# Row-group scores, one-tile mixing and two-tensor work on VectorE in a linear-attention, Fourier-mixing and feed-forward kernel

## The chip, the core and the metric

The kernel runs on one core of one Trainium2 chip. A core has five engines, each with its own instruction queue that is worked off strictly in order: TensorE (PE in the profile; its weight loads are listed apart as PEld), VectorE (DVE), ScalarE (ACT), GpSimd (POOL) and SyncE (SP), from whose queue most transfers are issued. [...] The metric is the device time of one execution in microseconds (us), lower is better.

## The reference

For 4 batches and 8 heads of width 48 a state of 48 x 48 is carried over 768 tokens; the result is mixed by a two-dimensional Fourier transform, normalised and sent through a feed-forward network:

```python
def _attn_ref(q, k, v, alpha):
    ...
    for t in range(S):
        state = alpha[:, :, t, :, None] * state + np.einsum('bhd,bhe->bhde', k[:, :, t], v[:, :, t])
        y[:, :, t] = np.einsum('bhd,bhde->bhe', q[:, :, t], state)

def _moe_ref(x, w_ch1, w_ch2):
    X = np.fft.fft(np.fft.fft(x, axis=1), axis=2)
    u = x + np.real(X)
    un = (u - mean(u)) / np.sqrt(var(u) + 1e-06)
    return u + np.maximum(un @ w_ch1, 0.0) @ w_ch2
```

Here `x` is the attention result with its 8 heads side by side: 768 tokens by 384. `w_ch1` is 384 x 1536, `w_ch2` 1536 x 384. Everything is float32.

## The kernel before

**Attention.** The 32 (batch, head) problems run as 16 pairs of two heads, four pairs to a batch. The two heads of a pair lie on rows 0 to 47 and 64 to 111 of the 112 used rows. For a pair, `attn_stages` gives these stages: `s1` makes running products of alpha by two scans on VectorE (tiles `al` and `w`, the latter being tag `w3`) and a product `first` of 112x384; `s2` and `s3` multiply them by k and q (`times`, two products of 112x768); `s4` transposes the k side (`kt`); `s5` makes the scores, k against q, in chunks of 128 tokens; `s6` makes and chains the states between chunks (`tt`); `s7` multiplies scores by v and adds the carried state; then `combine` does the first radix-3 step of the Fourier transform along tokens (tiles `sd`, then six parts `z`).

**Scores in two forms.** Pairs 0 to 6 (`pair < FR`, FR = 7) use `s5`: float32 matmuls of one head each, on 64 or 48 rows of the array. Pairs 7 to 15 use `s5r`: k and q are each split into a high and a low part in the one-pass float32r format (tile `qs`), q also masked by head (`hm`), and three matmuls on all 112 rows with both heads side by side (128x256) make a chunk. `s5r` costs ScalarE three and VectorE three instructions for each half of a pair ahead of the matmuls. Either way ScalarE copies the scores out of PSUM and GpSimd zeroes the upper triangle (`affine_select`).

**Mixing, norm, feed-forward.** `mix_stages` folds the six parts of `z` (`f2`; z lies in three `w3` tiles of two parts each, so each step of the fold is issued three times), transforms along tokens (`mk_s`) and channels (`mk_d`) on TensorE, and VectorE adds the results to `y`. `norm_stages` normalises, transposes on TensorE (`n2`), and splits into high and low parts `x`. `ffn_stages` runs 12 blocks of 128 hidden channels for each of two halves of a batch: 9 float32r matmuls 128x384 (`f<-x,wt`; order lists them as `f<-x,wt` or `f<-wt,h` with moving and fixed operand exchanged), ScalarE's relu, VectorE's low part, 9 matmuls back. The two halves of 4 batches make 1728 matmuls. The weights are turned from float64 words to float32r high and low parts on the chip (`wsplit`).

**What sets the order.** All instructions are first collected with a key, then `Plan.emit` places them one at a time: it simulates five clocks with the costs in `duration`, the latencies `LAT`, a port rule for VectorE and GpSimd (`port`, `held`, `SHARE`) and takes, on the engine that can start earliest, the ready instruction with the lowest key. Some operations may go to either of two engines (`FX`, with a bias `SLACK`). The order so found is each engine's queue; on the chip nothing is reordered. In the first 120 us of its own clock the plan fills TensorE's gaps with dummy matmuls on a zero tile (`f<-zero`), one for each 0.11 us of gap. Tiles come from numbered slots of a tag (`w3`: NW3 = 8, `qs`: 3, PSUM `a`: 3, `f1`: 2, `f2`: 3); taking a slot waits for its last user. Of batch 1, MIX and K1 place some stages among the mixing of batch 0, ahead of the first feed-forward.

## Time and profile before

| | |
|---|---|
| runs, median (lowest to highest) | 571.66 us (571.16 to 576.05), 3 runs |
| the profiled execution | 572.74 us, of which the trace's span 570.9 us and 1.84 us around it |
| mean granted TensorE clock | 0.946 |
| busy: PE, DVE, ACT, POOL | 534.1, 398.2, 195.6, 220.1 us |
| GpSimd's instructions | 255, of which 175 TENSOR_TENSOR and 64 affine selects |

The profiled execution is 1.08 us above the median of the runs. A busy TensorE is not TensorE at its peak: matmuls overlap in the pipe, dummies count as busy, and the clock was 0.5 in parts of the first 100 us. So the profile has to be read by stages: first until the first feed-forward matmul, then while feed-forward and the next batch's attention share the engines, and last the feed-forward of the last batch alone.

### The profile page before, as it was taken

The numbers are of one execution on the slowest core, as the hardware profiler recorded it, in microseconds if no ns is written. First come the engines' busy times: TensorE is split into PE (matmuls) and PEld (weight loads), VectorE is DVE, ScalarE is ACT, GpSimd is POOL, SyncE is SP. The second block draws the span as 40 slices with busy tenths as digits, with TensorE's granted clock in tenths as the row PEclk, the third lists the DMA queues.
The fourth block names the chain that finished last, engine by engine and source line by source line (L and its number), as shares of the span: only waits on it lengthen the run. The fifth ranks groups of instructions, "written<-read, shape, count | busy, mean of one in ns | idle before, by whom it ended". The sixth has DMA issues, their size and how long they took to land.

```text
span 570.9 us, 10199 instructions
## 1 busy us (share of the span) xinstructions
PE 534.1 (94%) x4018; PEld 510.9 (89%) x4018; DVE 398.2 (70%) x903; ACT 195.6 (34%) x428; POOL 220.1 (39%) x255
## 2 busy tenths in 40 slices
PE   7999879989898999998989999999999999999995
PEld 6888878978887989998979999988999999999995
DVE  7766796898999666999984679989755932412111
ACT  3354422345643522245643213255522121211110
POOL 2557584264758440055857202358770000000000
PEclk8575976999998999999999999999999999999998
DMA  8999080230200250112324300221011100100001
GB/s 223 276 363 270 21 284 15 75 95 1 69 2 2 70 153 1 47 37 78 97 64 142 124 1 1 91 64 29 2 56 29 42 1 0 43 0 27 17 0 48
DMA packets 16550, 42.23 MB, mean 74 GB/s; under 512 B 1904, under 2 KB 7088, under 8 KB 16496
## 3 DMA queue, kind: packets, MB, share of 16 engines
q1 hardware_dynamic: 15440, 39.08, 22.2%
q0 software_dynamic: 768, 2.36, 1.4%
q8 instruction: 34, 0.56, 0.4%
q14 instruction: 20, 0.16, 0.1%
q10 hardware_dynamic: 288, 0.07, 0.1%
HBM read 34.42 MB, written 7.08 MB: 73 GB/s over the span
## 4 chain that ended last, share of the span: by engine, by line
PE 62%; DVE 18%; POOL 7%; DMA 4%; issue 4%; ACT 2%; SPq 1%; POOLq 0%; ACTq 0%; DVEq 0%
PE f L464 42%; PE a L464 19%; DVE w L464 6%; POOL w L464 4%; DMA al<-in_alpha_dram 4%; DVE al L464 3%; POOL sd L464 2%; DVE h L464 2%; PE f L1146 2%; DVE qs L464 2%; DVE x L464 2%; DVE tt L464 1%; DVE y L464 1%; DMA scr<-y 1%; SPq L464 1%
## 5 line engine op out<-in xcount | busy, mean ns | idle before, releaser
L464 PE MATMUL f<-wt,h 128*128 128x384 f32 x864 | 178.4, 342 | 5.1 <-DVE h L464 5.1
L464 PE MATMUL f<-x,wt 128*128 128x384 f32 x864 | 179.0, 343 | 0.8 <-DVE x L464 0.8
L464 PEld LDWEIGHTS f<-wt,h 128*128 128x128 f32 x864 | 149.9, 188 | 7.8 <-DVE h L464 7.2
L464 PEld LDWEIGHTS f<-x,wt 128*128 128x128 f32 x864 | 152.0, 189 | 1.8 <-DVE x L464 1.2
L464 DVE SCALAR_TENSOR_TENSOR h<-f,h 128x384 fp32r<-128x384 f32 x96 | 53.1, 553 | 93.2 <-ACT h L211 92.2
L211 ACT ACTIVATE h<-f 128x384 fp32r<-128x384 f32 x96 | 47.1, 490 | 182.3 <-PE f L464 176.4
L464 POOL TENSOR_SCALAR_AFFINE_SELECT w<-w 128x512 f32<-128x512 f32 (+1 forms) x64 | 47.5, 765 | 44.3 <-ACT w L464 44.3
L464 POOL TENSOR_TENSOR w<-w,rec 112x384 f32<-112x384 f32 (+1 forms) x17 | 18.1, 1065 | 103.3 <-DVE mt L464 45.5
L464 PE MATMUL a<-vn,w 128*128 128x64 f32 x312 | 49.4, 288 | 3.3 <-POOL w L464 2.3
L464 PEld LDWEIGHTS a<-vn,w 128*128 128x128 f32 x312 | 45.1, 208 | 5.3 <-POOL w L464 3.5
L464 POOL TENSOR_TENSOR sd<-y,y 128x288 f32<-128x288 f32 x32 | 33.0, 1052 | 35.6 <-ACT y L464 30.8
L1146 PE MATMUL f<-zero 128*32 128x32 f32 x798 | 36.8, 210 | 3.5 <-ACT w L464 1.9
L464 ACT COPY w<-a 128x512 f32<-128x512 f32 (+6 forms) x58 | 26.2, 481 | 40.2 <-PE a L464 39.0
L1146 PEld LDWEIGHTS f<-zero 128*32 128x32 f32 x798 | 32.8, 125 | 7.6 <-ACT w L464 2.4
L464 DVE TENSOR_TENSOR y<-y,a 128x191 f32<-128x191 f32 (+2 forms) x96 | 28.6, 346 | 13.3 <-PE a L464 13.1
L464 DVE SCALAR_TENSOR_TENSOR tt<-tt,mt 112x96 f32<-112x96 f32 x64 | 35.5, 557 | 0.3
L464 PE MATMUL a<-cst,w 96*128 96x96 f32 (+10 forms) x267 | 34.2, 267 | 1.3 <-DVE w L464 1.2
L464 PEld LDWEIGHTS a<-cst,w 128*96 128x96 f32 (+7 forms) x267 | 32.0, 166 | 3.2 <-DVE w L464 2.2
L464 DVE TENSOR_TENSOR_SCAN al<-al,d 112x768 f32<-112x768 f32 (+1 forms) x17 | 34.6, 2037 | 0.1
L464 PE MATMUL a<-qs,qs 112*128 112x256 f32 x162 | 29.2, 292 | 4.7 <-DVE qs L464 4.7
L464 DVE TENSOR_TENSOR_SCAN w<-al,d 112x768 f32<-112x768 f32 (+1 forms) x17 | 32.3, 1902 | 0.2
L464 PE MATMUL a<-tt,w 112*128 112x96 f32 x134 | 30.4, 312 | 1.1 <-DVE d L464 1.1
(129 smaller groups left out, 737.5 us busy)
## 6 DMA issues: line engine op xcount, KB each, us to landing
kq<-in_kq_dram SPq DMA_DIRECT2D x13, 672.0 KB, 5.4
wt<-in_w_dram SPq DMA_DIRECT2D x8, 768.0 KB, 10.9
al<-in_alpha_dram SPq DMA_DIRECT2D x15, 336.0 KB, 9.7
out_dram<-y SPq DMA_DIRECT2D x24, 192.0 KB, 1.9
vn<-in_v_dram SPq DMA_DIRECT2D x14, 296.0 KB, 3.5
wt<-in_w_dram SPq DMA_DIRECT2D x8, 384.0 KB, 13.0
scr<-y SPq DMA_DIRECT2D x4, 576.0 KB, 3.9
wt<-in_kq_dram SPq DMA_DIRECT2D x2, 672.0 KB, 12.7
```

Source lines behind the costliest of these rows:

```text
L211: return lambda out, x: e.activation(out, x, AF.Relu)
L464: op.ins = op.fns[op.engine](*[real(a) for a in op.args], **{k: real(x) for k, x in op.kwargs.items()})
L1146: plan.idle = (lambda: nc.tensor.matmul(warm[2][0:32, 480:512], zero.real(), zero.real(), start=True, stop=True), 1.0, WARM, ("f2", 2))
```

## The change

- `s5r`, FR and the tag `qs` go; all 16 pairs use `s5`. In the plan a float32 matmul on at most 64 rows costs a fifth less (750 for 600).
- `combine`, `times` (`mul`) and `first` are given to VectorE alone. The weights' products (`wm`, `wd`) may still go to either engine, now with no slack for GpSimd.
- `z` becomes one tile of six parts, and so does the folded `f`: each step of the fold is one instruction over six parts in place of three over two. The blk-0 norm result uses `f` too. NW3 falls from 8 to 5.
- In the plan VectorE and GpSimd no longer slow one another by a share: an instruction with two wide SBUF inputs (or a constant) waits until the other engine's has ended.
- In the plan a matmul that is no feed-forward (`not u.fill`) counts its operands from other engines as ready MARGIN = 1.0 us later than the latencies say.

```diff
-NQS = 3
-FR = 7
-NW3 = 8
+NW3 = 5
+MARGIN = 1.0
...
-                return max(m, slow * n) / 600 + 0.004
+                p0, p1 = self.region(named["1"])[0:2]
+                return max(m, slow * n) / (750 if p1 - p0 <= GRP else 600) + 0.004
...
         if len(wide) > 1:
-            return "part"
-        return "whole" if wide and op.name in ("tensor_scalar", "tensor_copy", "copy") and "scalar1" in named else None
+            return True
+        return len(wide) > 0 and "scalar1" in named and not isinstance(named["scalar1"], View)
...
+        def finish(op, e):
+            t = max(clock[e], start(op, e))
+            return (max(t, held[other[e]]) if op.port and e in held else t) + op.durs[e]
...
-                op.dur += (SHARE if op.port == "part" else 1.0) * both
...
+                op.dur += max(0.0, held[other[op.engine]] - t)
+                held[op.engine] = t + op.dur
...
+                    if e == "PE" and op.engine != "PE" and not u.fill:
+                        lat += MARGIN
...
-SLACK = {'ACT': 2.0, 'DVE': 0.5, 'POOL': 5.0}
-FX = {'comb': 'G', 'mul': 'VG', 'first': 'G', 'wm': 'VG', 'wd': 'VG', ...
-SHARE = 0.5
+SLACK = {'ACT': 2.0, 'DVE': 0.5, 'POOL': 0}
+FX = {'comb': 'V', 'mul': 'V', 'first': 'V', 'wm': 'VG', 'wd': 'VG', ...
...
-        "qs": ([P, 776], F32R, NQS), "sd": ...
+        "z": ([P, 6, DM], F32, 1), "f": ([P, 6, DM], F32, 1), "sd": ...
...
-        def s5r():
...
-        return [s1, s2, s3, s4, s5 if pair < FR else s5r, s6, s7, lambda: combine(...)]
+        return [s1, s2, s3, s4, s5, s6, s7, lambda: combine(...)]
...
-        z = [x[:, c0 : c0 + w] for x in zt[0]]
+        z = [zt[:, i, c0 : c0 + w] for i in range(6)]
...
-            for z, f in zip(zp, fp):
-                ze, zo = f[:, :, 0 : HM + 1], f[:, :, HM:DM]
-                E.tensor_add(ze[:, :, 1:HM], z[:, :, 1:HM], z[:, :, DM - 1 : HM : -1])
...
+            z, f = zt, plan.tile("f")
+            ze, zo = f[:, :, 0 : HM + 1], f[:, :, HM:DM]
+            E.tensor_add(ze[:, :, 1:HM], z[:, :, 1:HM], z[:, :, DM - 1 : HM : -1])
...
-                uw = [plan.tile("qs").bitcast(F32) if state["start"] else w3() for _ in range(2)]
+                uw = plan.tile("f")
```

The instruction counts follow: VectorE gains 32 `sd` (128x288) and 96 `z` (128x96) two-tensor instructions of `combine`, 19 products with k or q (18 of 112x768, one of 112x384), 17 `first` and 10 products of 128x768 of the weights; it loses 54 instructions with `qs` and two thirds of the fold's. GpSimd keeps the 64 `affine_select`, the 12 gathers and one weight product. ScalarE loses 54 instructions with `qs`. On TensorE 162 matmuls `a<-qs,qs` become 108 of `a<-w,al`.

The first place is the start-up, where the first pair of batch 0 is combined. Names are tiles with their buffer numbers: `sd`, `y`, `al`, `w` (tag `w3`), `d` (the scans' second input). On GpSimd's queue before:

```order
L464 TENSOR_TENSOR w_5_6_71<-w_5_6_71,rec 112x6x64
L464 TENSOR_TENSOR w_5_6_71<-wt_0_65_130,w_5_6_71 112x768
L464 TENSOR_TENSOR sd_13_78<-y_23_88,y_24_89 128x288 x2
L464 TENSOR_TENSOR w_6_7_72<-sd_13_78 128x96
L464 TENSOR_TENSOR w_7_8_73<-sd_13_78 128x96
L464 TENSOR_TENSOR w_6_7_72<-sd_13_78,w_6_7_72 128x96
L464 TENSOR_TENSOR w_3_92_515<-sd_13_78 128x96 x2
L464 TENSOR_TENSOR w_7_8_73<-sd_13_78,w_3_92_515 128x96
L464 AFFINE_SELECT w_0_93_517<-w_0_93_517 128x384 x2
```

The same work on VectorE's queue now, ahead of the scan of the fourth pair:

```order
L465 TENSOR_TENSOR al_38_103<-wt_0_61_126,al_38_103 112x768
L465 TENSOR_TENSOR sd_9_74<-y_19_84,y_20_85 128x288 x2
L465 TENSOR_TENSOR z_7_72<-sd_9_74 128x96 x2
L465 TENSOR_TENSOR z_7_72<-sd_9_74,z_7_72 128x96
L465 TENSOR_TENSOR z_7_72<-sd_9_74 128x96
L465 SCALAR_TENSOR_TENSOR z_7_72<-z_7_72,sd_9_74 128x96
L465 TENSOR_TENSOR z_7_72<-sd_9_74 128x96
L465 TENSOR_TENSOR z_7_72<-sd_9_74,z_7_72 128x96
L465 SCALAR_TENSOR_TENSOR w_1_91_536<-al_39_104,d_137 112x768
L465 SCALAR_TENSOR_TENSOR z_7_72<-z_7_72,sd_9_74 128x96
```

The combination stands between VectorE's own scans now, and GpSimd's queue goes from one `affine_select` to the next.

The second place is ScalarE's queue ahead of the first feed-forward matmul (`r` are the norm's small tiles, `x` the feed-forward's input, `c` and `bad` belong to the check of a later pair's alpha, `mh` and `y` to later pairs' states and results). Before:

```order
L464 ACTIVATE r_4_38_103<-mv_33_98,ceps 128x3
L464 ACTIVATE mh_136<-mt_140,hm 112x5 x2
L464 COPY y_27_92<-f_0_162_1123 128x3x96
L464 ACTIVATE c_0_183_1355,bad<-al_180_1307,cm_144 112x768
L464 COPY w_2_188_1371<-f_1_165_1148 128x384
L464 COPY w_2_188_1371<-f_0_171_1174 128x384
L464 COPY w_0_190_1398<-f_1_167_1156 128x384
L464 CAST x_191_1400<-f_1_189_1394 128x384
```

And now:

```order
L465 ACTIVATE r_1_31_96<-mv_28_93,ceps 128x3
L465 ACTIVATE r_4_34_99<-mv_29_94,ceps 128x3
L465 CAST x_146_1264<-f_0_143_1248 128x384
L465 CAST x_147_1267<-f_0_144_1250 128x384
L465 CAST x_150_1281<-f_1_145_1252 128x384
L465 ACTIVATE x_151_1285<-b_0_113_727 128x768
```

The states, results and the check of pairs 5 and 6 no longer stand ahead of the casts of `x`; they come after the feed-forward has begun. In TensorE's queue 212 attention and mixing matmuls (and 472 dummies) stand ahead of the first feed-forward matmul now, 273 (and 396) before.

The third place is TensorE's queue at the scores of one of the later pairs. Before (pair 7, float32r, both heads in one matmul):

```order
L464 MATMUL a_276_1901<-tt_134,w_1_178_1295 128x2x48
L464 MATMUL a_286_1970<-qs_12_77,qs_284_1960 128x256
L464 MATMUL a_286_1970<-qs_281_1937,qs_284_1960 128x256
L464 MATMUL a_288_1976<-qs_12_77,qs_284_1960 128x256
L464 MATMUL a_288_1976<-qs_281_1937,qs_284_1960 128x256
```

And now (pair 8, float32, one head on its own rows in each; two heads in turn write two PSUM tiles, or one head stands alone):

```order
L465 MATMUL a_376_2638<-w_4_317_2275,al_168_1348 128x128 x2
L465 MATMUL a_377_2642<-w_4_317_2275,al_168_1348 128x128 x2
L465 MATMUL a_378_2649<-w_4_317_2275,al_168_1348 128x128 x3
L465 MATMUL f_0_372_2618<-x_355_2539,wt_0_118_768 128x384
L465 MATMUL a_380_2658<-w_4_317_2275,al_168_1348 128x128 x3
L465 MATMUL a_383_2667<-vn_284_2050,kt_375_2631 112x96 x5
```

Over the nine later pairs 54 of the 108 score matmuls stand next to one of the other head, 54 alone, in 23 groups between other work.

More of the change, by code (lines that the diff above doesn't have):

```diff
@@ L328, in port @@
         if op.engine == "POOL":
-            return None if "dma" in op.name else "part"
-        if op.engine != "DVE" or op.name == "memset":
-            return None
+            return "dma" not in op.name
+        if op.name == "memset":
+            return False
         inputs = [a for k, a in named.items() if k != "out" and isinstance(a, View)]
@@ L365, in emit @@
         order = []
-        held = {"DVE": (0.0, 0.0), "POOL": (0.0, 0.0)}
+        held = {"DVE": 0.0, "POOL": 0.0}
+        other = {"DVE": "POOL", "POOL": "DVE"}
         def start(op, e):
@@ L396, in emit @@
                     if len(op.engines) > 1:
-                        done = max(now, t) + op.durs[e] - SLACK[e]
-                        if any(max(clock[o], start(op, o)) + op.durs[o] < done for o in op.engines if o != e):
+                        if any(finish(op, o) < finish(op, e) - SLACK[e] for o in op.engines if o != e):
                             continue
@@ L425, in emit @@
             if op.port and op.engine in held:
-                other = "POOL" if op.engine == "DVE" else "DVE"
-                a, b = held[other]
-                both = max(0.0, min(b, t + op.dur) - max(a, t))
-                op.dur += (SHARE if op.port == "part" else 1.0) * both
-                if other == "POOL":
-                    clock[other] += SHARE * both
-                held[op.engine] = (t, t + op.dur)
+                op.dur += max(0.0, held[other[op.engine]] - t)
+                held[op.engine] = t + op.dur
             end = t + op.dur
@@ L729, in s5 @@
                     G.affine_select(out=xs, in_=xs, pattern=[[0, 3], [1, P]], compare_op=ALU.is_ge, fill=0.0, base=0, channel_multiplier=-1)
-        def s5r():
-            e["X"] = []
-            for h2 in range(2):
-                sl = slice(h2 * DM, (h2 + 1) * DM)
-                X = w3()[:, 0:S].rearrange("p (c two n) -> p two c n", two=2, c=3)
-                e["X"].append(X)
-                qh, ql, kk = (plan.tile("qs")[0:CW, 0:S] for _ in range(3))
-                kh, kl = kk[:, 0:DM], kk[:, DM:S]
-                qh, ql = (x.rearrange("p (c h t) -> p h c t", c=3, h=2) for x in (qh, ql))
-                q_, k_ = e["A"][0:CW, sl].rearrange("p (c t) -> p c t", c=3), R(slice(0, CW), sl.start, sl.stop)
-                for hd in range(2):
-                    A.activation(qh[:, hd], q_, AF.Copy, scale=hm[0:CW, hd : hd + 1])
-                    V.scalar_tensor_tensor(
-                        out=ql[:, hd], in0=q_, scalar=hm[0:CW, hd : hd + 1], in1=qh[:, hd].bitcast(F32), op0=ALU.mult, op1=ALU.subtract
-                    )
-                A.copy(kh, k_)
-                FL["kl"].tensor_sub(kl, k_, kh.bitcast(F32))
-                for c0, c1 in ((0, 2), (2, 3)):
-                    pc = psa()
-                    for c in range(c0, c1):
-                        cs = slice(c * P, (c + 1) * P)
-                        for n, (kx, qx) in enumerate(((kh, qh), (kh, ql), (kl, qh))):
-                            T.matmul(pc[:, (c - c0) * 2 * P : (c - c0 + 1) * 2 * P], kx[:, cs], qx[:, :, c], start=n == 0, stop=n == 2)
-                    xs = X[:, :, c0:c1].rearrange("p h c t -> p c h t")
-                    FL["ev"].copy(xs, pc[:, 0 : (c1 - c0) * 2 * P].rearrange("p (c h t) -> p c h t", c=c1 - c0, h=2))
-                    G.affine_select(out=xs, in_=xs, pattern=[[0, 2 * (c1 - c0)], [1, P]], compare_op=ALU.is_ge, fill=0.0, base=0, channel_multiplier=-1)
         def s6():
@@ L792, in s7 @@
                 FL["ev"].copy(ytiles[h2][:, :, hp * 2 * D : (hp + 1) * 2 * D].rearrange("p a (h e) -> p a h e", h=2), yo)
-        return [s1, s2, s3, s4, s5 if pair < FR else s5r, s6, s7, lambda: combine(*mixed(), hp * 2 * D, 2 * D, FL["comb"])]
+        return [s1, s2, s3, s4, s5, s6, s7, lambda: combine(*mixed(), hp * 2 * D, 2 * D, FL["comb"])]
     def early():
         return plan.tile("x").bitcast(F32) if state["start"] else w3()
-    def w6(new=None):
-        t = [(new or w3)() for _ in range(3)]
-        return [t[i // 2][:, (i % 2) * DM : (i % 2 + 1) * DM] for i in range(6)], [x[:, 0:S] for x in t]
     def combine(ytiles, zt, c0, w, E=None):
@@ L944, in n1 @@
             if blk == 0:
-                uw = [plan.tile("qs").bitcast(F32) if state["start"] else w3() for _ in range(2)]
-                un = [uw[0][:, 0:DM], uw[0][:, DM:S], uw[1][:, 0:DM]]
+                uw = plan.tile("f")
+                un = [uw[:, m] for m in range(3)]
             else:
@@ L1030, in mixed @@
             if b not in sequence:
-                sequence[b] = ([plan.tile("y") for _ in range(2)], w6())
+                sequence[b] = ([plan.tile("y") for _ in range(2)], plan.tile("z"))
             return sequence[b]
@@ L1221, in general_rest @@
                 SY.dma_start(ytiles[h2][:, a].rearrange("p (g n) -> p g n", g=NP2), yv[h2, :, a])
-        zt = w6()
+        zt = plan.tile("z")
         for g in range(NP2):
```

28 lines of the change are left out of this document (12 added, 16 removed).

## The prediction

> **What bounds the kernel now.** I read the profile in this order: the windows view cut at the stages, then the timelines of VectorE, ScalarE and TensorE before the first feed-forward matmul, then the waits of TensorE, then the groups by form for prices. The windows view gives for each stretch its length and the busy time (with instruction counts) of PE, PEld, DVE, ACT and POOL, then the granted TensorE clock, DMA share and GB/s.
>
> ```profile
> span 570.9 us, 10199 instructions
> ...
> 0.00:90.00 90.00, 78.62 (x891) 71.76 (x892) 68.12 (x158) 34.77 (x74) 53.45 (x66) 0.73 0.75 230
> 90.00:125.00 35.00, 32.52 (x398) 28.79 (x398) 27.42 (x87) 11.44 (x28) 11.60 (x10) 0.91 0.23 69
> 125.00:243.00 118.00, 109.85 (x704) 105.00 (x702) 100.05 (x191) 48.48 (x92) 54.93 (x60) 0.99 0.14 43
> 243.00:460.00 217.00, 208.74 (x1431) 201.79 (x1432) 176.48 (x420) 83.94 (x200) 100.11 (x120) 1.00 0.18 56
> 460.00:571.00 111.00, 104.33 (x600) 103.58 (x599) 26.17 (x50) 17.02 (x36) 0.00 (x0) 0.98 0.05 17
> ```
>
> From 125 us on TensorE is the bound: 109.85 of 118 us, 208.74 of 217, and at the end 104.33 of 111, where nothing of the change runs. Before 125 us there is no feed-forward work. TensorE's busy time there is largely dummies and waits at a clock of 0.73, and the stretch is as long as a chain through all engines. Its pieces, first on VectorE (start, length, instruction, and in brackets the wait ahead of it and who ended it):
>
> ```profile
> 19.17 1.68 DVE L464 SCALAR_TENSOR_TENSOR tt<-tt,mt 112x96 f32<-112x96 f32 x1
> ...
> 35.61 0.31 DVE L464 SCALAR_TENSOR_TENSOR tt<-tt,mt 112x96 f32<-112x96 f32 x1
> ...
> 46.83 1.86 DVE L464 SCALAR_TENSOR_TENSOR tt<-tt,mt 112x96 f32<-112x96 f32 x1
> ...
> 55.44 0.96 DVE L464 TENSOR_TENSOR wt<-h,wt 128x768 fp32r<-128x768 f32 x1 [5.19 <-ACT wt L464]
> ...
> 67.67 0.42 DVE L464 SCALAR_TENSOR_TENSOR w<-w,sd 128x96 f32<-128x96 f32 x1 [2.47 <-POOL w L464]
> ...
> 75.58 2.24 DVE L464 TENSOR_TENSOR_SCAN al<-al,d 112x768 f32<-112x768 f32 x1
> ...
> 88.43 1.29 DVE L464 TENSOR_TENSOR w<-x 128x192 f32<-128x192 f32 x6
> ...
> 100.33 1.41 DVE L464 TENSOR_TENSOR y<-y,f 128x193 f32<-128x193 f32 x5 [5.89 <-PE f L464]
> ...
> 114.94 1.26 DVE L464 TENSOR_SCALAR h<-y,mv,r 128x384 f32<-128x384 f32 x3
> ```
>
> The fold of batch 0 ends at 89.7, the transforms come back at 100.3, and the norm is through at 116.2. Then ScalarE and TensorE:
>
> ```profile
> 119.36 0.49 ACT L464 ACTIVATE mh<-mt,hm 112x5 f32<-112x5 f32 x2 [6.62 <-DVE mt L464]
> ...
> 122.45 0.94 ACT L464 ACTIVATE c<-al,cm 112x768 uint8<-112x768 uint8 x1 [1.77 <-DMA al<-in_alpha_dram]
> ...
> 124.48 1.32 ACT L464 CAST x<-f 128x384 fp32r<-128x384 f32 x3
> ```
>
> ```profile
> 125.40 0.44 PE L464 MATMUL f<-x,wt 128*128 128x384 f32 x1
> ```
>
> Between the norm's end and the first feed-forward matmul lie 9.2 us, most of them ScalarE waiting for a later pair's `mt` and for a transfer, with the casts of `x` queued behind.
>
> **The change, part by part.** Prices on VectorE come from these groups (count, then busy us and mean ns of one):
>
> ```profile
> L464 DVE SCALAR_TENSOR_TENSOR qs<-w,hm,qs 112x384 fp32r<-112x384 f32 x36 | 25.4, 729 | 8.0 <-ACT qs L464 8.0
> L464 DVE SCALAR_TENSOR_TENSOR tt<-tt,mt 112x96 f32<-112x96 f32 x64 | 35.5, 557 | 0.3
> L464 DVE TENSOR_TENSOR y<-y,a 128x191 f32<-128x191 f32 x66 | 20.4, 346 | 0.0
> L464 DVE TENSOR_TENSOR y<-y,f 128x384 f32<-128x384 f32 x36 | 18.7, 550 | 6.6 <-PE f L464 6.6
> L464 DVE TENSOR_TENSOR qs<-al,qs 112x384 fp32r<-112x384 f32 x18 | 13.6, 757 | 0.1
> L464 DVE TENSOR_TENSOR w<-w 128x382 f32<-128x382 f32 x18 | 9.6, 560 | 2.5 <-POOL w L464 1.6 <-issue 0.8
> L464 DVE TENSOR_TENSOR w<-w 128x192 f32<-128x192 f32 x18 | 6.4, 357 | 0.2
> L464 DVE TENSOR_TENSOR wt<-h,wt 128x768 fp32r<-128x768 f32 x2 | 1.9, 947 | 5.2 <-ACT wt L464 5.2
> ```
>
> 191 elements take 0.346 and 384 take 0.550, so 0.144 plus 1.06 ns per element: 0.25 for 96, 0.45 for 288, 0.55 for 384; 768 take 0.95. Over the whole run VectorE gains 32 x 0.45 + 96 x 0.25 + 18 x 0.95 + 18 x 0.55 + 10 x 0.95 = 75 us. It loses 39 us with `qs` (25.4 + 13.6), and about 3 us a batch of the fold: three times two instructions at 0.56 and four near 0.35 become two of 1146 elements (1.36) and four near 0.75, 9.2 against 6.2 with the small copies (0.16 each). It also loses the time in which GpSimd slows it: the same `tt` instruction took 0.31 alone, 1.68 and 1.86 beside this:
>
> ```profile
> 46.30 2.28 POOL L464 TENSOR_TENSOR w<-wt,w 112x768 f32<-112x768 f32 x1
> ```
>
> It began at 46.83 and ended 0.11 us after GpSimd's product. [...] GpSimd keeps its 64 affine selects, so some of this stays.
>
> Step A, up to the first feed-forward matmul. VectorE's fold ends at 89.7 now. Added ahead of it: four combines at 2 x 0.45 + 6 x 0.25 = 2.4, four `first` (2.4) and products with k and q that GpSimd had (3.4), together +15.4. Gone: the two waits that GpSimd's products ended, 5.2 and 2.5 (the 5.2 is named for ScalarE, whose copy waited for GpSimd's part of the weight), -7.7; stretched instructions such as 1.68, 1.86 and the scan of 2.24, about -8 in all; the fold's saving, -3; the scans and products of pair 4, which the new order puts behind the fold, -6; and about 6 of the two other waits of this stretch, for TensorE behind a GpSimd product and for the first weights, which VectorE will reach later. Sum -15: fold at 74. The way through the transforms (10.6) stays, since pair 4's work now lies under it; adds and norm (116.2 - 100.3 = 15.9, with a few `tt` among them) lose about 1; and the last 9.2 become about 3, since the casts follow the norm directly. So the first feed-forward matmul comes near 102 instead of 125.4: -23. Ends: -10, if TensorE at a clock of 0.73 is what really paces the first 90 us, and -31, if it warms up with denser work. The 76 further dummies are priced by this row:
>
> ```profile
> 58.87 1.39 PE L1146 MATMUL f<-zero 128*32 128x32 f32 x38
> ```
>
> 76 x 0.037 = 2.8 us if none of them falls into a gap, 0 if all do; I take 0, since the plan sets them only where it sees a gap.
>
> Step B. That early start is bought: 61 attention matmuls (273 - 212) now come after it, with two pairs' VectorE work. These rows price TensorE's side, and the scores:
>
> ```profile
> 144.89 1.60 PE L464 MATMUL a<-w,al 64*128 64x128 f32 x18
> 146.42 1.49 PE L464 MATMUL f<-wt,h 128*128 128x384 f32 x7
> ...
> 174.40 0.93 PE L464 MATMUL a<-w,al 48*128 48x128 f32 x6
> 175.26 1.22 PE L464 MATMUL a<-vn,kt 128*112 128x96 f32 x10
> ...
> 189.05 1.31 PE L464 MATMUL a<-qs,qs 112*128 112x256 f32 x9
> 190.21 0.34 PE L464 MATMUL f<-x,wt 128*128 128x384 f32 x1
> ```
>
> A float32 matmul leaves two records. Ten records `a<-vn,kt`, five matmuls, take some 1.06 of 1.22 us, 0.21 each, so +12.8 us.
>
> Step C, scores. From start to start, three matmuls of one head took 175.26 - 174.40 = 0.86. Nine took 146.42 - 144.89 = 1.53, of which six ran as three concurrent couples: six places. So a place costs (1.53 - 0.86) / 3 = 0.22 and a group 0.19 besides. The nine later pairs have 27 + 54 = 81 places in 23 groups: 18.1 + 4.4 = 22.5. In the old form nine matmuls took 1.16, so 162 take 20.9. Difference +2; I take +4, with a like loss on the neighbour's side for half of the groups. Ends -3 (no loss at all) and +6.
>
> Step D, waits of TensorE and its weight loads:
>
> ```profile
> PEld f L464 <- DVE h L464: 7.2, 7, 2.0
> PEld a L464 <- DVE qs L464: 6.8, 8, 1.5
> PEld a L464 <- POOL w L464: 3.5, 5, 1.2
> PEld f L464 <- POOL w L464: 2.4, 2, 2.1
> ```
>
> The 6.8 go with `qs`; of the 5.9 for GpSimd's triangles (the figures are the sum, the count and the longest) the margin of 1 us should hide some. I take -8, ends -13 and 0: the margin only helps while TensorE has feed-forward work to put first, and that is so from 125 to 460 us.
>
> Step E, VectorE during the feed-forward of batch 0 (125 to 243). It was busy for 100 of 118 us. It now gets two pairs' scans and states (14), four combines (10), its share of `first`, products and weights (15), and loses qs (4) and about 13 of stretched time: 122. TensorE's own need there is 109.85 + 12.8 less its waits, about 119. Two full queues that wait on one another cost something: +4, ends 0 and +15. What is then late is the low part of `h`, queued behind scans of 1.75 us.
>
> Sum: -23 + 12.8 + 4 - 8 + 4 = -10.2. Against the profiled execution (572.74, that is the span of 570.9 and 1.84 around it) this gives 562.5. The median of the runs is 1.1 lower, so I say 562 for the median.
>
> **The rivals.**
> Rival 1, no change: the start-up is paced by TensorE's clock and not by VectorE. For it speaks 0.73 in the first row of the windows, and busy 78.62 of 90; against it, that VectorE's own waits name GpSimd. Step A is then -10, the sum +3: 575, or 570 with step D at its lower end.
> Rival 2, slower: VectorE becomes the bound of the stretch of step E. If affine selects stretch its two-input work as much as GpSimd's products did, 122 becomes 135 and with the idle share it has now (18 of 118) 150 us; step E is then near +25 and the whole 583. It decides from the point where VectorE is busy for over 97% of the stretch. For it speaks that it takes on 75 us; against it, that it sheds 50 and more.
> Rival 3, the row groups cost a drain each. Per group 0.19 inside and, at its upper end, as much again on both neighbours, 23 groups x 0.57 = 13 instead of 6.6: 568. [...] It speaks against this change and is a size, not a sign.
>
> **How the numbers follow.** Forecast 0.62: 562, its own range 550 to 566. Rivals 1 and 3 together 0.20, at 567 to 576 (1 has 0.13, 3 has 0.07). Rival 2 and its like 0.18, 577 to 590. A measurement of this kernel tells about 1% from no change, so faster means under 566 and slower over 577. Low end: steps A and D at their lower ends and E at 0 give 547. High end: half of rival 2 is taken in, 580.
>
> **What would show it.** Right: the first `f<-x,wt` between 95 and 108; no VectorE wait for GpSimd over 1 us before it; `tt` at a mean near 0.35 (557 ns in the groups above); far less busy time of GpSimd, and less of ScalarE. Step C right: 216 records of later scores in about 23 us. Wrong: a first feed-forward matmul after 115, TensorE waits for `h` well above 7.2 us, or a stretch of batch 0's feed-forward longer than 135 us.

## The result and the profile after

| | before | changed |
|---|---|---|
| median of 20 runs (lowest to highest) | 571.67 us (570.32 to 576.05) | 569.81 us (564.69 to 577.36) |
| profiled execution, its span | 572.74, 570.9 us | 569.96, 568.2 us |
| ratio to before, 95% interval | | 0.9935 [0.991, 0.9959] |

The change makes the kernel 0.65% faster, where 1.7% was forecast. Disturbed runs are left out of the ratios but not of the medians, which is why a ratio can lie away from the quotient of two medians. The runs of the changed kernel lie wider apart than those of before: from 562.9 us of span at a mean TensorE clock of 0.952 to 575.6 at 0.936.

The windows view of the changed kernel, cut near its stages (length, busy time of PE, PEld, DVE, ACT, POOL, then the granted clock, DMA share, GB/s), with its line on the span ahead of it:

```profile
span 568.2 us, 10337 instructions
...
0.00:90.00 90.00, 81.90 (x1000) 75.76 (x1000) 63.86 (x171) 34.36 (x72) 17.79 (x23) 0.77 0.74 230
90.00:103.00 13.00, 12.20 (x288) 11.47 (x286) 12.93 (x48) 2.44 (x5) 0.00 (x0) 1.00 0.01 3
103.00:125.00 22.00, 17.75 (x117) 15.24 (x117) 17.28 (x43) 10.23 (x22) 4.14 (x4) 0.77 0.16 48
125.00:243.00 118.00, 113.17 (x734) 109.58 (x735) 100.38 (x234) 43.01 (x87) 14.72 (x16) 0.96 0.17 53
243.00:460.00 217.00, 214.66 (x1504) 207.02 (x1503) 150.38 (x413) 63.99 (x154) 26.95 (x38) 1.00 0.18 57
460.00:568.00 108.00, 101.51 (x583) 100.78 (x581) 25.25 (x48) 16.52 (x34) 0.00 (x0) 0.99 0.05 18
```

From 243 us on TensorE is nearly full: 214.66 of 217 us, 208.74 before. Between 103 and 243 us the clock is below that of before, 0.77 and 0.96 (1.00 and 0.99 in the same stretches). The path to the first feed-forward matmul, from the timelines of VectorE, ScalarE and TensorE:

```profile
77.22 1.34 DVE L465 TENSOR_TENSOR f<-z 128x1146 f32<-128x1146 f32 x1
...
81.08 2.91 DVE L465 TENSOR_TENSOR z<-f 128x576 f32<-128x576 f32 x6
...
92.91 1.14 DVE L465 TENSOR_TENSOR y<-y,a 128x193 f32<-128x193 f32 x4
...
107.28 1.26 DVE L465 TENSOR_SCALAR h<-y,mv,r 128x384 f32<-128x384 f32 x3
```

```profile
106.36 1.24 ACT L465 CAST x<-f 128x384 fp32r<-128x384 f32 x3 [2.24 <-PE f L465]
```

```profile
111.02 3.25 PE L465 MATMUL f<-x,wt 128*128 128x384 f32 x9
```

Fold over at 84.0 (89.7 before), adds from 92.9 (100.3), norm through at 108.5 (116.2), first feed-forward matmul at 111.0 (125.4). VectorE's own instructions come near the prices, 0.35, 0.25 and 1.36 (groups by form: count, busy us, mean ns):

```profile
L465 DVE SCALAR_TENSOR_TENSOR tt<-tt,mt 112x96 f32<-112x96 f32 x64 | 21.1, 331 | 0.5
...
L465 DVE TENSOR_TENSOR z<-sd 128x96 f32<-128x96 f32 x64 | 17.4, 294 | 0.0
...
L465 DVE TENSOR_TENSOR f<-z 128x1146 f32<-128x1146 f32 x8 | 10.6, 1345 | 0.1
```

`tt` went from 557 to 331 ns. VectorE is busy for 370.1 us where it was 398.2, GpSimd for 63.6 where it was 220.1.

For every kernel of this study the table gives when the 1st, 433rd, 865th and 1297th feed-forward matmul (the first of each batch) and the last began, in its profiled execution, and when batch 0's `y` was sent to DRAM (the transfer `scr<-y`, the end of batch 0's attention). These are counted in the traces. The second column has what the profiled execution took, and in brackets the median of the kernel's runs.

| kernel | profiled (median) | scr<-y | 1st | 433rd | 865th | 1297th | last |
|---|---|---|---|---|---|---|---|
| before | 572.7 (571.7) | 72.4 | 125.4 | 241.9 | 368.7 | 488.3 | 564.0 |
| changed | 570.0 (569.8) | 72.9 | 111.0 | 244.0 | 366.4 | 485.2 | 562.0 |
| m0_no_margin | 575.5 (570.0) | 76.1 | 113.2 | 253.8 | 373.2 | 491.6 | 567.5 |
| bv_engines_only | 580.4 (580.1) | 83.8 | 122.7 | 263.1 | 379.8 | 496.1 | 571.7 |
| bs5_scores_only | 585.3 (588.0) | 73.2 | 126.3 | 243.3 | 378.4 | 501.0 | 576.6 |
| mix13_less_ahead | 589.2 (587.2) | 84.2 | 126.3 | 260.8 | 385.4 | 504.2 | 581.0 |
| bd_before_more_dummies | 571.5 (576.3) | 71.6 | 122.6 | 238.7 | 366.1 | 487.0 | 562.7 |
| m0d_no_margin_more_dummies | 568.1 (565.4) | 69.0 | 107.9 | 246.8 | 365.7 | 484.1 | 560.0 |
| ald_late_margin_more_dummies | 572.2 (580.0) | 76.8 | 115.1 | 246.0 | 368.4 | 487.3 | 564.1 |
| aw0_no_dummies | 571.4 (563.9) | 76.2 | 111.8 | 245.3 | 367.7 | 486.6 | 563.4 |
| bw0_before_no_dummies | 569.8 (570.1) | 72.5 | 124.2 | 240.2 | 365.6 | 485.3 | 560.9 |
| b1d_other_psum | 562.0 (564.5) | 74.7 | 109.7 | 238.4 | 358.4 | 477.2 | 554.0 |
| b1dw0_other_psum_no_dummies | 569.6 (564.0) | 77.8 | 113.0 | 243.7 | 365.8 | 484.6 | 561.4 |
| dose_psum_and_dosed_dummies | 563.5 (564.6) | 75.6 | 110.0 | 239.4 | 359.3 | 478.1 | 554.9 |

The first two rows hold the question. The feed-forward starts 14.4 us earlier, and at the 433rd matmul the changed kernel is 2.1 us behind. TensorE's waits between 111 and 243 us (us in total, times, longest) show one large one:

```profile
PE f L465 <- DVE tt L465: 6.7, 1, 6.7
PE a L465 <- ACT kt L465: 0.6, 2, 0.3
```

Its place, on TensorE, then on VectorE, then on ScalarE:

```profile
120.42 1.82 PE L465 MATMUL f<-x,wt 128*128 128x384 f32 x9
128.95 0.74 PE L465 MATMUL f<-tt,w 112*128 112x96 f32 x2 [6.71 <-DVE tt L465]
```

```profile
121.62 0.96 DVE L465 TENSOR_TENSOR wt<-x,wt 128x768 fp32r<-128x768 f32 x1 [2.55 <-ACT wt L465]
...
124.70 1.75 DVE L465 TENSOR_TENSOR_SCAN al<-al,d 112x768 f32<-112x768 f32 x1
...
128.25 0.65 DVE L465 TENSOR_TENSOR tt<-f,mh 112x480 f32<-112x480 f32 x1
```

```profile
119.83 0.94 ACT L465 ACTIVATE c<-al,cm 112x768 uint8<-112x768 uint8 x1 [2.53 <-DMA al<-in_alpha_dram]
```

TensorE's queue has a state matmul of batch 1 next, whose `tt` stands on VectorE behind weights and a scan; VectorE waited 2.55 us for ScalarE's cast of a weight, which stood behind the check of an alpha that had not landed. No feed-forward matmul stands in between on TensorE. What followed this hole is in the windows view of the changed kernel in steps of 3.4 us (PE's busy time is the second number, the clock the third from the end):

```profile
119.20:122.60 3.40, 3.04 (x23) 2.72 (x21) 0.98 (x2) 2.14 (x5) 0.25 (x1) 1.00 0.46 136
122.60:126.00 3.40, 0.00 (x0) 0.00 (x0) 3.40 (x4) 1.61 (x3) 0.00 (x0) 0.99 0.00 0
126.00:129.40 3.40, 0.45 (x2) 0.45 (x3) 3.40 (x10) 0.95 (x3) 0.00 (x0) 0.50 0.00 0
129.40:132.80 3.40, 3.40 (x15) 3.40 (x15) 3.39 (x11) 0.89 (x3) 0.00 (x0) 0.50 0.00 0
132.80:136.30 3.50, 3.50 (x14) 3.50 (x13) 2.62 (x3) 0.49 (x1) 0.00 (x0) 0.52 0.00 0
136.30:139.70 3.40, 3.40 (x24) 3.37 (x24) 3.40 (x9) 0.00 (x0) 0.00 (x0) 1.00 0.01 2
```

Here the stretch without a matmul is followed by three at half clock (0.50, 0.50 and 0.52), and from start to next start a feed-forward matmul `f<-x,wt` takes 0.320 us at half clock in this trace where it takes 0.176 at full. The hole of 6.7 us so costs more than its length. It is not all that is lost here: the clock had already been at half from 105.5 to 115.7 us, behind a stretch in which TensorE was busy for 1.32 of 3.4 us, where it stood at 1.00 from 103 us on before.

### The profile page after: what moved, and what is told of

It is laid out like the page before. It is cut to its first block, busy times and chain, and to the rows that moved or that the text cites. A ratio compares the mean times of both kernels' runs of the same rounds, so it can differ in the third digit from the quotient of the medians.

```text
span 568.2 us, 10337 instructions
## 1 busy us (share of the span) xinstructions
PE 541.2 (95%) x4220; PEld 519.8 (91%) x4220; DVE 370.1 (65%) x952; ACT 170.6 (30%) x373; POOL 63.6 (11%) x81
## 4 chain that ended last, share of the span: by engine, by line
PE 86%; DVE 7%; DMA 3%; ACT 2%; issue 1%; SPq 1%; ACTq 0%
PE f L465 58%; PE a L465 25%; DMA al<-in_alpha_dram 3%; PE f L1111 3%; DVE y L465 2%; DVE x L465 1%; DVE wt L465 1%; SPq L465 1%; DVE st L465 1%; ACT c L465 1%; DVE z L465 0%; DVE tt L465 0%; DVE h L465 0%; DVE w L465 0%; DVE al L465 0%
## 5 line engine op out<-in xcount | busy, mean ns | idle before, releaser
L465 POOL TENSOR_SCALAR_AFFINE_SELECT w<-w 128x384 f32<-128x384 f32 x64 | 42.4, 682 | 290.9 <-ACT w L465 290.8
L1111 PEld LDWEIGHTS f<-zero 128*32 128x32 f32 x946 | 37.3, 124 | 4.9 <-issue 2.0
L465 ACT COPY w<-a 128x384 f32<-128x384 f32 (+4 forms) x58 | 26.2, 481 | 35.2 <-PE a L465 33.9
L465 PE MATMUL a<-w,al 48*128 48x128 f32 (+1 forms) x276 | 33.7, 296 | 0.0
L465 PEld LDWEIGHTS a<-w,al 48*128 48x128 f32 (+1 forms) x276 | 27.5, 193 | 4.1 <-issue 1.6
L465 DVE TENSOR_TENSOR sd<-y,y 128x288 f32<-128x288 f32 x32 | 13.2, 453 | 25.0 <-ACT y L465 25.0
L465 DVE TENSOR_TENSOR_SCAN al<-al,d 112x768 f32<-112x768 f32 (+1 forms) x17 | 28.2, 1656 | 0.0
L465 DVE TENSOR_TENSOR y<-y,f 128x384 f32<-128x384 f32 (+2 forms) x44 | 21.2, 515 | 6.9 <-PE f L465 6.7
L465 PEld LDWEIGHTS a<-tt,w 112*128 112x128 f32 x134 | 22.6, 203 | 0.9 <-issue 0.2
L465 POOL DMA_INDIRECT y<-scr,rows x12 | 18.1, 1510 | 46.1 <-DMA scr<-y 33.5
## 6 DMA issues: line engine op xcount, KB each, us to landing
wt<-in_w_dram SPq DMA_DIRECT2D x8, 768.0 KB, 10.6
```

The costliest lines, as they stand in the source:

```text
L465: op.ins = op.fns[op.engine](*[real(a) for a in op.args], **{k: real(x) for k, x in op.kwargs.items()})
L1111: plan.idle = (lambda: nc.tensor.matmul(warm[2][0:32, 480:512], zero.real(), zero.real(), start=True, stop=True), 1.0, WARM, ("f2", 2))
```

## The experiments

**One part at a time: the margin.** The changed kernel with

```diff
-MARGIN = 1.0
+MARGIN = 0.0
```

> The changed kernel with the margin at 0 (nothing else). If the margin does what step D priced (it hides TensorE's waits for the triangles and the scores' copies, 5.9 us before), those waits return, 4 to 8 us more: 574 to 578 against 569.8. Rival: the margin costs at the start, where ScalarE's first copy of kt stands behind the check of pair 1's alpha and comes at 12.5 us instead of 7.7; then the first feed-forward matmul comes 2 to 5 us earlier than 111.0 and the time is 564 to 568.

570.0 us (10 runs), ratio 0.9928 [0.9886, 0.997]: the same as with the margin, and neither expectation came. The waits that the margin was to hide are not back. The windows view of before, of the changed kernel and of this one, from 165 us on:

```profile
165.00:243.00 78.00, 73.14 (x473) 70.34 (x472) 62.40 (x148) 24.54 (x54) 30.07 (x33) 0.98 0.17 52
243.00:366.00 123.00, 117.07 (x785) 112.97 (x785) 103.64 (x240) 47.99 (x115) 58.38 (x65) 1.00 0.23 68
```

```profile
165.00:243.00 78.00, 77.69 (x519) 75.78 (x518) 69.23 (x163) 26.39 (x55) 12.27 (x12) 1.00 0.16 49
243.00:366.00 123.00, 120.66 (x831) 116.28 (x830) 88.11 (x239) 37.47 (x90) 13.38 (x19) 1.00 0.23 69
```

```profile
165.00:243.00 78.00, 77.97 (x519) 76.03 (x518) 69.30 (x154) 30.47 (x59) 13.40 (x13) 1.00 0.18 54
243.00:366.00 123.00, 122.76 (x849) 119.11 (x848) 95.42 (x262) 37.94 (x93) 13.46 (x19) 1.00 0.24 74
```

TensorE is idle for 4.86 and 5.93 us in these two stretches before, for 0.31 and 2.34 with the margin, for 0.03 and 0.24 without it. So it was not the margin that took the waits away; what did, the next two runs show. The rival was right about the start of the queue (ScalarE's first `kt` at 7.58 instead of 12.49 us), but the store of `y` came no earlier in the execution that was profiled, which took 575.5 us.

**The engine split alone**, in the kernel before:

```diff
-SLACK = {'ACT': 2.0, 'DVE': 0.5, 'POOL': 5.0}
-FX = {'comb': 'G', 'mul': 'VG', 'first': 'G', ...
+SLACK = {'ACT': 2.0, 'DVE': 0.5, 'POOL': 0}
+FX = {'comb': 'V', 'mul': 'V', 'first': 'V', ...
```

> The kernel before, with only the engine split changed (combine, products with k and q, and first on VectorE alone, no slack for GpSimd). If VectorE's work off GpSimd is what brings the start forward, the first feed-forward matmul comes near 112 instead of 125.4 and GpSimd's stretching falls from 60 us to under 25; with qs still on VectorE (39 us) the stretch of batch 0 is longer by as much and the whole is 568 to 576. Rival: the earlier start comes from the one-tile fold; then the first feed-forward matmul stays behind 118.

Median 580.14 us of 11 runs (570.23 to 585.48), ratio 0.998 [0.9935, 1.0024]. VectorE was relieved as expected:

```profile
L464 DVE SCALAR_TENSOR_TENSOR tt<-tt,mt 112x96 f32<-112x96 f32 x64 | 20.9, 338 | 0.5
```

Each of VectorE's instructions counted against the median of its operation and shape, the time above it falls from 62.2 to 18.8 us (the sum over the trace; 10.5 in the changed kernel). TensorE's waits in the later batches went with it, though this kernel keeps `qs` and has no margin. The windows view of before, of this kernel and of the next one, which has no `qs` but GpSimd's old load:

```profile
243.00:378.00 135.00, 128.87 (x874) 124.46 (x875) 112.67 (x258) 54.64 (x131) 60.28 (x68) 1.00 0.22 66
```

```profile
243.00:378.00 135.00, 135.00 (x914) 133.94 (x912) 119.78 (x337) 52.45 (x125) 14.10 (x19) 1.00 0.22 68
```

```profile
243.00:378.00 135.00, 130.54 (x829) 124.95 (x828) 91.12 (x219) 37.27 (x91) 53.36 (x64) 0.92 0.21 63
```

From 165 to 486 us TensorE is idle for 13.1 us before, 2.1 here and 10.6 in the next kernel. So the waits went with the engine split, or the order planned with it, and not with `qs`. From the 433rd to the 1297th feed-forward matmul this kernel takes 233.0 us, fewer than before (246.4) and than the changed kernel (241.2, or 237.8 without the margin).

What it gains there it lost in the start: the store of `y` came at 83.8 us, 11.4 later than before, at a clock of 0.61 up to 72 us, and the first feed-forward matmul at 122.7. In this execution, of 580.4 us, freeing VectorE of GpSimd did not by itself bring the start forward. Five of the 11 runs took 570.2 to 572.6 us, and what their start was like no trace shows.

**The scores alone**, in the kernel before:

```diff
-FR = 7
+FR = 16
```

> The kernel before with float32 scores for all 16 pairs (FR = 16), nothing else. Step C: 81 places and 23 groups cost 22.5 us against 20.9, and the waits for qs (6.8 us) go: 566 to 571. Rival, a drain for each group beside feed-forward work: 13 us instead of 4.4 for the groups, 572 to 578; then the feed-forward matmuls next to score groups start later than 0.19 us behind them.

587.97 us (4 runs), ratio 1.0283 [1.0193, 1.0373]: slower than either expectation. Up to the 433rd matmul it is 1.4 us behind before, in the next batch it loses 8.3 (135.1 for 126.8), then 3.0. The timelines of VectorE, GpSimd and TensorE in this kernel, where the 8.3 us begin:

```profile
254.48 3.79 DVE L464 TENSOR_TENSOR_SCAN al<-al,d 112x768 f32<-112x768 f32 x1
258.19 0.63 DVE L464 TENSOR_TENSOR tt<-a,mh 112x480 f32<-112x480 f32 x1
258.75 1.63 DVE L464 TENSOR_TENSOR d<-al 112x12 int32<-112x12 int32 x1
```

```profile
255.19 3.39 POOL L464 TENSOR_SCALAR_AFFINE_SELECT w<-w 128x384 f32<-128x384 f32 x4
258.55 1.80 POOL L464 TENSOR_TENSOR w<-kq,w 112x768 f32<-112x768 f32 x1
```

```profile
258.87 0.46 PE L464 MATMUL a<-tt,w 112*128 112x96 f32 x2 [1.19 <-DVE d L464]
...
260.67 0.74 PE L464 MATMUL a<-tt,w 112*128 112x96 f32 x2 [0.92 <-DVE al L464]
```

A scan of 1.75 us takes 3.79 beside a product of GpSimd and its triangles (beside triangles alone scans take up to 2.07 in this trace and 1.95 in the changed kernel), and a small instruction `d<-al`, 0.18 at its median, takes 1.63 and ends with GpSimd's product; two states come late, and the clock falls to half for six stretches of 3.4 us between 260 and 298 us (mean clock 0.92 from 243 to 378 us, 1.00 before). In the changed kernel, where GpSimd does little but zero triangles, the same batch takes 122.4 us. So float32 scores cost 2.8% at GpSimd's old load. That they gain anything at the new one no run shows: the engine split with the old scores was faster in these batches (233.0 for 241.2 us above), and the changed kernel with the old scores was not tried.

**Less of batch 1 ahead of the feed-forward**, in the changed kernel:

```diff
-MIX = (5, 2, 2, 3, 3)
+MIX = (5, 2, 2, 3, 1)
```

> The changed kernel with 13 of batch 1's units ahead of the feed-forward instead of 15 (the scores of pair 5's neighbour and its transposes go behind; these then take only the three a tiles). Theory 1: the 6.7 us in which TensorE stood at 122 to 129, and the half clock that followed, come from units that were put ahead and overran the start of the feed-forward, holding its PSUM tiles; the hole is then under 3 us and the time 560 to 565. Rival, VectorE's queue is what is late (weights and scans before tt): TensorE stands as long at another place and the time is 567 to 572.

587.23 us (4 runs), ratio 1.0192 [1.0104, 1.028]: both missed. The plan's whole order came out differently: `scr<-y` at 84.2, the first feed-forward matmul at 126.3. It tells nothing of the hole, and shows that a new order can move the first feed-forward matmul by as much as the change does (15.3 us later here, 14.4 earlier there).

**The clock.** With the traces of these six kernels theory C was formed: the clock paces the start. The dummies alone were changed; a dummy stands only where the plan sees a gap, and no other instruction moves:

```diff
-DUMMY = 0.11
+DUMMY = 0.07
...
-                for _ in range(int((t - max(clock["PE"], self.idle[1])) / DUMMY)):
+                for _ in range(int((t - max(clock["PE"], self.idle[1])) / (0.11 if t < 7.2 else 0.05 if t < 12.0 else DUMMY))):
```

> The kernel before with more dummies in the gaps that its plan already fills (one for 0.05 us of gap between 7.2 and 12 us of the plan's clock, for 0.07 after that, in place of 0.11); every other instruction keeps its order. [...] Then the clock stays 1.0 through most of the first 70 us, batch 0's y goes to DRAM before 62 us (72.4 now), the first feed-forward matmul comes near 112 (125.4) and the whole is 555 to 562. Rival: the start is a chain through VectorE, ScalarE and transfers; the store of y moves by less than 4 us, the whole stays 568 to 574.

576.32 us (10 runs), ratio 1.0046 [1.0014, 1.0078]. The clock was 0.87 up to 72 us instead of 0.74, yet `scr<-y` came 0.8 us earlier only. Theory C fell in this form. Up to 72 us the dummies took 24.9 us of TensorE's time (17.7 before), and work 38.5 (46.5), from start to next start: the clock's gain was paid to the dummies.

The same dummies in the changed kernel with margin 0:

> The changed kernel with margin 0 and the same rule for dummies. Theory C: store of y before 62 us (72.9 in the changed kernel), first feed-forward matmul under 101, the whole 550 to 558, and the spread between runs (563 to 577 without) under 6 us, since it comes from the clock. If the change is worth what the prediction said once the clock is out of it, it is 7 to 12 us below the kernel before with the same dummies; if TensorE's work between 110 and 165 us is the bound, 0 to 4 us below.

565.43 us (4 runs, 562.96 to 568.1), ratio 0.9848 [0.9788, 0.9908]. The clock was 0.93 up to 72 us, dummies 31.2 us, work 35.1; `scr<-y` at 69.0, the best of all, but not below 62. The four runs lie within 5.1 us, too few to tell of the spread.

The same dummies in the changed kernel, with its margin of 1 us from 20 us of the plan on:

```diff
-                    if e == "PE" and op.engine != "PE" and not u.fill:
+                    if e == "PE" and op.engine != "PE" and not u.fill and t > 20.0:
```

> The changed kernel with the margin only from 20 us of the plan's clock on, and the same rule for dummies. Against the run with margin 0 this tells what the margin is worth with the clock out of it: by step D 4 to 8 us faster (waits of TensorE for triangles and copies hidden), by the rival (the margin only reorders, TensorE is full from 165 us on either way) within 3 us.

Three runs at 572.2 to 585.9 us, and one of 2913 us that nothing here explains. None of them is faster than the four with margin 0, so again no gain from the margin.

**No dummies**, in both kernels, first in the changed one:

```diff
-WARM = 120.0
+WARM = 0.0
```

> The changed kernel without any dummy matmul (936 of TensorE's records go, all of them before 120 us; nothing else moves). Up to 72 us TensorE was idle for 3.9 us only: 21.8 us went to dummies and 45.4 to work. Theory D: the dummies stand in the in-order queue ahead of work that is ready, since at half clock TensorE is behind the plan, and it is this queue that paces the start; without them batch 0's y goes to DRAM 8 to 20 us earlier than 72.9, and the first feed-forward matmul comes at 92 to 103 (111.0) although the clock stays at 0.5 until then; the whole 555 to 566. Rival, the chain through the other engines paces and the dummies only fill: store of y at 70 or later, TensorE idle for over 15 us up to there; the whole 568 to 580, since the feed-forward then begins at half clock.

563.94 us (6 runs), ratio 0.9827 [0.9766, 0.9888]: in the range of theory D, but not by its way. The store of `y` came later, at 76.2, and the profiled execution, at 571.4 us, is one of the two long ones of the six, so where the 6 us of the others come from its trace does not show. It does show what paces the start:

```profile
13.41 1.44 PE L465 MATMUL f<-vn,kt 128*112 128x96 f32 x6 [5.53 <-ACT kt L465]
...
41.69 0.74 PE L465 MATMUL a<-tt,w 112*128 112x96 f32 x2 [3.01 <-DVE tt L465]
...
75.06 0.69 PE L465 MATMUL f<-tt,w 112*128 112x96 f32 x2
...
84.84 4.88 PE L465 MATMUL f<-cst,z 128*97 128x65 f32 x24 [9.10 <-issue]
```

From 13.4 to 75.7 us TensorE works without a pause but for 3.2 us, at durations near twice those of full clock (`f<-tt,w` 0.69 for 0.41). The clock column cannot be used here: it reads 1.00 up to 72 us, since the trace's clock record begins at 89.5 us.

The kernel before without dummies:

> The kernel before without any dummy matmul. Theory D: store of y 5 to 15 us before 72.4; the first feed-forward matmul 112 to 120 (125.4), whole 560 to 568. Rival: store at 70 or later, whole 570 to 582. The difference to the changed kernel without dummies is the change without the dummies' 76 more: 2 to 5 us if the dummies are what it lost in the start, 8 to 14 us if it is the other way round and they held the kernel before back less.

570.09 us (10 runs), ratio 0.9953 [0.991, 0.9997]. Store at 72.5, as the rival said. From 13.4 to 72 us TensorE was idle for 10.2 us, 6.9 of them in one wait for a tile of GpSimd's, where the changed kernel without dummies was idle for 3.2. So in the kernel before other engines hold the start as well; in the changed one, in the execution that was profiled, it is nearly TensorE alone.

**The hole.** In the plan the units of batch 1 that are put ahead may take any PSUM tile (`a`, `f1`, `f2`), and where they overrun the first feed-forward matmul, they hold one of its two `f1` tiles until `tt` has been read. With a tiles only, from the tenth unit on:

```diff
+B1 = ("a",)
...
-            return plan.tile(start_tags[state["i"] % 8])
+            return plan.tile(start_tags[state["i"] % 8] if not state.get("b1") else B1[state["i"] % len(B1)])
...
+        state["b1"] = done >= 9
         write(order1[done : done + n], K1 + 0.01 * done, ...
```

> The changed kernel, but the units of batch 1 that are put ahead of the feed-forward take only the three a tiles of PSUM from the tenth unit on, so that the two f1 tiles are free for the feed-forward. Theory E: of the 14.4 us that the earlier start brought, most was lost because TensorE had nothing to issue for 6.7 us (waiting for tt behind the weights on VectorE, feed-forward blocks not yet placed for want of an f1 tile) and then ran 10 us at half clock; with the tiles free the first 108 feed-forward matmuls take under 35 us (52 now) and the 432nd comes 5 to 10 us earlier than 242.6, the whole 558 to 565. Rival: VectorE and TensorE have the same work to do up to there in any order; the wait comes back before the 432nd, which stays within 3 us of 242.6, the whole 566 to 573.

564.51 us (4 runs; 562.0, 562.7, 566.3 and 578.3), ratio 0.9877 [0.9805, 0.9948]. Theory E held. The first 108 feed-forward matmuls take 24.8 us (52.1 in the changed kernel), the 432nd begins at 228.6 (242.6), and the last is 8.0 us earlier. With other tiles the plan also orders anew from about the first feed-forward matmul on (1098 of TensorE's 3274 records other than dummies stand at another place), so tiles and order changed together. The windows view of the changed kernel, then of this one:

```profile
111.00:125.00 14.00, 11.24 (x68) 10.22 (x67) 9.29 (x16) 6.10 (x15) 4.14 (x4) 0.83 0.25 75
125.00:165.00 40.00, 35.48 (x217) 33.80 (x218) 31.15 (x72) 16.62 (x33) 2.45 (x4) 0.87 0.20 59
```

```profile
111.00:125.00 14.00, 13.75 (x92) 12.90 (x91) 13.68 (x23) 7.66 (x17) 3.08 (x4) 1.00 0.25 75
125.00:165.00 40.00, 39.80 (x263) 37.76 (x262) 33.88 (x78) 18.41 (x36) 2.05 (x4) 1.00 0.20 59
```

TensorE's 7.3 idle us between 111 and 165 become 0.5, and the clock stays at 1.00. VectorE was busy for 7.1 us more there (47.56 for 40.44) in the same time, so it was not the bound.

Not all of the gain lasts. Between the 432nd and the 433rd matmul lie 9.8 us (1.4 in the changed kernel). TensorE has run out of batch 0's feed-forward, and its waits there (us in total, times, longest) are for batch 1's norm, whose small tile is `r`:

```profile
PE a L466 <- DVE r L466: 2.1, 1, 2.1
PE a L466 <- issue: 1.5, 1, 1.5
```

The clock is at half for 10.2 us from 230.6 us on. Of the 14.0 us gained at the 432nd matmul 5.6 are left at the 433rd. So the rival's wait did come back, just behind the place where the rival looked for it.

Other tiles and `WARM = 0.0` together:

> The same without dummies. Without dummies alone the changed kernel took 563.9; if the two act at different places (start, and the stretch after 111 us) they add: 553 to 560 by theory E, 562 to 567 by its rival.

564.0 us (4 runs, 560.96 to 569.62), ratio 0.985 [0.9781, 0.9919]. By its median the two do not add.

**Dummies by dose.** Other PSUM tiles, the late margin, and fewer dummies in gaps under 2 us:

```diff
+NEED = 0.60
...
-                for _ in range(int((t - max(clock["PE"], self.idle[1])) / DUMMY)):
+                act = sum(x for q, x in seen if q > t - 3.4)
+                gap = t - max(clock["PE"], self.idle[1])
+                full = int(gap / (0.11 if t < 7.2 else 0.05 if t < 12.0 else 0.08))
+                for _ in range(full if gap > 2.0 or t < 12.0 else min(full, max(0, math.ceil((NEED * 3.4 - act) / 0.053)))):
+                    seen.append((t, 0.053))
...
```

> The kernel with the other PSUM tiles for batch 1's units, the margin only from 20 us of the plan's clock on, and dummies dosed: in gaps of the plan under 2 us only as many as lift the row-weighted streaming of the last 3.4 us to 0.6, in longer gaps and before 12 us filling them. Theory C (TensorE's queue paces the start; at half clock with its work, at full clock with its dummies): with the clock mostly at 1.0 and dummies up to 72 us under 23 us (28.2 in the run with more dummies and late margin) the store of batch 0's y comes at 62 to 69 (72.9) and the whole at 550 to 559. Rival: other engines' chain stops it at 70 or later; the whole 560 to 566.

564.61 us (10 runs), ratio 0.9864 [0.9814, 0.9914]. Dummies still took 24.9 us up to 72, the clock was 0.81 there, and the store came at 75.6. The condition of theory C was not met, so it neither stands nor falls by this run. Five versions of the changed kernel (without dummies; margin 0 with more dummies; other PSUM tiles; these without dummies; these with dosed dummies) take 564 to 565.5 us, with intervals wholly under the kernel before. Only the first two have intervals apart from the changed kernel's own (0.991 to 0.9959), and among the five all overlap.

## Why the prediction was right or wrong

The direction was right, the range of 547 to 580 holds the result, and the size was wrong: 562 was forecast, 569.8 came. By the times of the table (1st, 433rd, last feed-forward matmul), step by step:

| step | forecast | measured |
|---|---|---|
| A, to the first feed-forward matmul | -23 | -14.4 |
| B and E, from there to the 433rd | +12.8 and +4 | +16.5 |
| C and D, from there to the last | +4 and -8 | -4.1 |
| sum | -10.2 | -2.0 (-2.7 with the tail) |

**Step A failed**, in its sentence "Sum -15: fold at 74". The fold ended at 84.0, 5.7 us earlier than before. The other terms of the step came: the transforms 8.9 instead of 10.6 us, adds and norm 15.6 (15.9), and the way from the norm to the first matmul 2.5 where 9.2 had been and "about 3" was forecast. The step took the waits and stretched instructions that VectorE loses for time that the path loses. They were not on the path: batch 0's `y` leaves at 72.9 us (72.4 before), and TensorE's queue has few gaps up to there. The windows view up to 72 us, of before and of the changed kernel:

```profile
0.00:72.00 72.00, 64.17 (x685) 58.66 (x686) 51.43 (x118) 30.42 (x65) 38.32 (x53) 0.74 0.77 229
```

```profile
0.00:72.00 72.00, 67.10 (x754) 61.18 (x754) 47.16 (x139) 29.49 (x63) 9.10 (x20) 0.76 0.75 229
```

VectorE's busy time fell from 51.43 to 47.16 us and GpSimd's from 38.32 to 9.10; TensorE's rose. The step also put the 76 further dummies at 0, with 2.8 us as the most they could cost. A dummy leaves two records (`f<-zero` has 152 more ahead of the first feed-forward matmul), so its row gives 5.6; up to 72 us the dummies took 21.8 us of TensorE's time where they had taken 17.7. This is rival 1's mechanism, which had 0.13 and, with step D at its lower end, gave 570: the row for it, busy 78.62 of 90 at a clock of 0.73, stood in the prediction, and was set aside for VectorE's waits that name GpSimd. The rival was worded too narrowly, though. It is not the clock alone: without dummies TensorE is full with work, idle for 3.2 us from 13.4 to 75.7 at durations near twice those of full clock, and at 0.87 to 0.93 it is full with work and dummies (more dummies). A form with full clock and few dummies, that would show what is left without either, was not reached, so that TensorE paces the start is borne out by these runs and not settled. What held the kernel before is open as well: without dummies its TensorE had gaps, and the store stayed at 72.5.

**Step B and E** came out at their sum by luck, for it was another mechanism than the one described. No full queues waiting on one another, and no low part of `h` late: TensorE's wait for `h` is gone. Instead one hole of 6.7 us with half clock behind it. Other PSUM tiles, and the order that came with them, take it away and give 5.6 us back by the 433rd matmul and 8.0 by the last. Rival 2 did not come: VectorE was busy for 100.38 of 118 us, where the step had 122, and under the 97% from which it would have decided. (Its 150 us is a slip: 135 with the idle share of 18 in 118 is 159.)

**Steps C and D** came out near their sum. From 165 to 486 us TensorE's idle time fell from 13.1 to 2.9 us, more than the 8 taken, but by neither of the two causes that the step named: not by the margin (m0_no_margin: 0.5 us idle without it), and not by the end of `qs` (bv_engines_only: 2.1 with `qs`; bs5_scores_only: 10.6 without). The later scores' 216 records take 22.3 us to the next start, as the mark of about 23 said. What the groups cost at their edges was priced a little low. Where one stands amid feed-forward, the matmul ahead of it lasts 0.266 instead of 0.176 us to the next start, the group's first 0.213 for 0.111, its last 0.202, the feed-forward matmul behind 0.281 (medians of the trace). That is 0.385 a group, where the step had 0.19 and as much again at the neighbours of half of them, 0.29, and rival 3 at its upper end 0.57. With what the neighbours lose, the nine later pairs take 27.4 us, where `qs` counted in the same way took 22.9, or 21.3 by itself: +4.5 to +6 for the +4 taken. The cost is of rival 3's kind and nearer to the step's size, and the trace has it at entry (0.19 of the 0.385) and at exit alike; that it is a drain no run shows.

Of the marks for right and wrong: no wait of VectorE for GpSimd over 1 us before the first feed-forward matmul, `tt` at 331 ns, GpSimd at 63.6 us, and the 216 records came; the first feed-forward matmul at 111.0 fell between the two marks, and batch 0's feed-forward, 133.0 us long, stayed just under its mark of 135.

## What to carry to other kernels

An engine's waits and stretched instructions are worth what the path loses, so before they are added up, find the engine whose queue has no gap in that stretch. Fillers in that queue are not free: in the kernel before, up to 72 us, more of them delayed the work behind them as much as the higher clock sped it up (7.2 us more for dummies, 8.0 less for work, at a clock of 0.87 for 0.74). When work is pulled ahead across a phase border, look at which buffers of the next phase it still holds at the border. A new order from a planner came out up to 11 us later here (batch 0's `y` at 84.2 for 72.9), so a part of a change is better tried in a form that keeps the order, as the runs with more or no dummies did, than in one that plans anew, as the others did. And a change of several parts can hold one that costs: the engine split took TensorE's waits away by itself, and the new scores were slower in the only run that had them alone.
